# Fifteen small loads of 1 to 15 partitions behind the last row of wo, into a tile that nothing reads

## The chip, the cores and the metric

The kernel runs on one core of a Trainium2 chip. The metric is the device time of that core in microseconds (us), the median of the runs shown. The core has five engines with an instruction stream each: TensorE (PE), VectorE (DVE), ScalarE (ACT), GpSimd (POOL) and SyncE (SP). SP computes nothing here; it issues nearly all the transfers (DMAs) between the large memory (HBM) and the on-chip memory (SBUF).

## The reference

One token `x` of 1024 numbers passes through two branches that are added to it:

```python
xn = _layernorm(x, axis=-1)
return x + _A_ref(xn, A_k_cache, A_v_cache, A_wq, A_wo) + _B_ref(xn, B_w1, B_b1, B_w2, B_b2)
```

Branch A is attention over the last 4096 positions of a cache, with 32 query heads of 128 that share 4 key and value heads: `q = x @ wq`, scores, softmax, the weighted sum over `v`, and `@ wo`. Branch B is a layernorm and an MLP, `gelu(y @ w1 + b1) @ w2 + b2`, with a hidden width of 3584. Everything is bf16. The weights and the two cache windows are 39.86 MB, read once; the result is 1024 numbers.

## The kernel before, in words

With a single token every product is a vector by a matrix, so the kernel streams the matrices through SBUF and uses each once. Four large buffers of 128 partitions by 32 KB (the pool `ring`) take the matrices in the order K window, wq in two halves, w1 in two halves, V window, w2 in two halves and wo in two halves. One more use of a buffer, `kt_scr`, holds the transposed K. A matrix is loaded into a buffer that an earlier one gives back, so from w1 on SP waits, ahead of most loads, for the matmuls or copies that read that buffer last.

PE does the vector products with one column of `x` (or of the hidden vector) as the weight and 512 columns of the matrix as the moving side. DVE and ACT rearrange K (L186, L200, L202). Scores, softmax and the attention output follow (L276 to L332). The last part is the output projection: the rows of w2 and wo are 28 and 32 chunks of 128 x 1024 that are accumulated into `accf` (L341), all but the last four. Those four go into a second accumulator `acct` (L357), so that what was gathered before can be copied out while they still arrive. The last half of wo is loaded in pieces of 8, 4, 2, 1 and 1 rows per partition (L229) for the same reason. DVE and ACT write the sum into `res` (L361, L362), and two stores of one row each bring it to HBM: L364 from SP and L365 from ACT.

Tile, the framework in which the kernel is written, gives each instruction the waits that its tiles need and decides in which order instructions stand in each engine's stream. A load carries a wait for the readers of the buffer, and also for earlier writers of the same bytes. Each transfer adds to one of eight counters when it has landed, taken in turn, and a wait is a wait for a count. At the end of the program SP waits for all eight counters and for the other engines, and then the engines meet in a barrier (L391).

The pool `consts` gives each tile its own place for the whole run.

Of the kernel before, what the change touches and what calls it, by code (L numbers as in the profile page):

```python
# [9 lines left out]
BF16 = mybir.dt.bfloat16  # L10
# [6 lines left out]
def kernel(  # L17
# [14 lines left out]
    nc = tc.nc  # L32
# [21 lines left out]
    consts = ctx.enter_context(tc.tile_pool(name="consts", bufs=1))  # L54
# [135 lines left out]
    for g in range(Hkv):  # L190
        T4 = scr[:, g, :].rearrange("p (c a j) -> p c a j", a=4, j=32)
        k = 0
# [30 lines left out]
    wo_v = A_wo.rearrange("(p c) n -> p c n", p=P)  # L223
    for i, cuts in enumerate([[0, 16], [0, 8, 12, 14, 15, 16]]):
# [4 lines left out]
            nc.sync.dma_start(out=tv[:, a:b, :], in_=wo_v[:, nr * i + a:nr * i + b, :])  # L229
        chunk_src += [("o", nr * i + r, tv[:, r, :]) for r in range(nr)]  # L230


    for i, w3 in enumerate(wq_tiles):
        for r in range(4):
# [161 lines left out]
```

## Time and profile before

| What | Value |
| --- | --- |
| time, median of 2 runs | 101.78 us (101.76 to 101.81) |
| span of the profiled execution, first to last instruction | 100.0 us |
| what lies outside the span (101.78 - 100.0) | 1.78 us |
| instructions | 970 |
| moved by DMA | 39.92 MB, mean 399 GB/s |
| busy: PE, DVE, ACT, POOL | 51%, 50%, 34%, 4% |
| mean granted TensorE clock | 0.778 |

The page gives the profiled execution no time of its own beyond its span; the difference to the median, 1.78 us, is what lies before the first and after the last instruction. Times in the profile are counted from the start of the span. "SPq" is SP's instruction stream. A row of the form `L229 SPq DMA_DIRECT2D` is the time for which SP was busy issuing a transfer, not the transfer itself. DMA queues: `q1` carries what SP issues, `q10` what ACT issues, `q8` and `q14` fetch instructions. A transfer consists of packets, and a view of a short stretch says how many packets began in it, on which queue, how many of them were small, and how much time they took as a share of the time of 16 DMA engines.

### The profile page before, as it was taken

Reading aid. Unit: us, or ns where it says so; the run is one execution under the profiler, and the core shown is the slowest. Engines: PE = TensorE matmul, PEld = TensorE weight load, DVE = VectorE, ACT = ScalarE, POOL = GpSimd, SP = SyncE. Lnnn points to the kernel's source line nnn. Section 1 sums busy time; section 2 is a strip of 40 time slices with the busy share of each in tenths; the row PEclk is TensorE's granted clock in tenths of the full one; section 3 lists DMA queues with packets and bytes.
Section 4 is the critical chain, followed back from the end, with each engine's and each line's share of the span. In section 5 each row is a group of like instructions: output and inputs, shape, how many; then the busy total and the mean of one; then the engine's idle time right before and its main releaser. Section 6 shows DMA issues by size and latency. Waiting matters only on the chain.

```text
span 100.0 us, 970 instructions
## 1 busy us (share of the span) xinstructions
PE 51.2 (51%) x365; PEld 20.0 (20%) x365; DVE 49.7 (50%) x92; ACT 34.1 (34%) x37; POOL 3.8 (4%) x16
## 2 busy tenths in 40 slices
PE   0065200008500940193892935999469950199980
PEld 0042200002100310031530322334123410033320
DVE  5445499999999999997125115410450000000021
ACT  5000002999999999962001044400000000000010
POOL 6005200000000000000000000000000000000000
PEclk9999999999995579555555555559985998557999
DMA  2999999999999999998999999999999999999920
GB/s 26 394 420 426 491 488 472 419 419 419 432 419 393 401 500 382 413 482 378 390 429 426 429 531 390 413 477 390 459 447 426 419 432 419 406 419 411 401 73 1
DMA packets 2878, 39.92 MB, mean 399 GB/s; under 512 B 309, under 2 KB 311, under 8 KB 698
## 3 DMA queue, kind: packets, MB, share of 16 engines
q1 hardware_dynamic: 2866, 39.85, 93.6%
q8 instruction: 3, 0.05, 0.2%
q10 hardware_dynamic: 8, 0.01, 0.0%
q14 instruction: 1, 0.01, 0.0%
HBM read 39.86 MB, written 0.00 MB: 398 GB/s over the span
## 4 chain that ended last, share of the span: by engine, by line
DVE 38%; DMA 24%; PE 21%; issue 9%; POOL 3%; ACT 2%; SPq 1%; POOLq 1%; ACTq 0%
DMA wo<-in_A_wo_dram 24%; DVE kt_scr L186 17%; DVE kT L202 16%; PE o_all L320 10%; PE sp L276 4%; PE acch L258 3%; ACT e L298 1%; DVE eTb L300 1%; PE qT_ps L262 1%; DVE m_loc L284 1%; PE acct L357 1%; SPq L229 1%; DVE q_sb L241 1%; POOLq L391 1%; POOL spread L110 1%
## 5 line engine op out<-in xcount | busy, mean ns | idle before, releaser
L200 ACT COPY kT<-kt_scr 32x1024 bf16<-32x1024 bf16 x26 | 27.1, 1042 | 14.8 <-DVE kt_scr L186 14.5
L186 DVE STREAM_TRANSPOSE kt_scr<-k_sb 128x4096 bf16<-128x4096 bf16 x4 | 17.4, 4411 | 0.0
L238 PE MATMUL accq<-wq,xnT 128*1 128x512 bf16 x64 | 7.1, 622 | 18.3 <-DMA wq<-in_A_wq_dram 18.3
L202 DVE COPY kT<-kt_scr 32x1024 bf16<-32x1024 bf16 x38 | 15.9, 419 | 0.5
L346 DVE COPY bulk<-accf 33x320 f32<-33x320 f32 x1 | 0.5, 483 | 21.9 <-ACT bulk L345 21.9
L341 PE MATMUL accf<-wo,o 128*1 128x512 bf16 x56 | 8.3, 459 | 6.0 <-DMA wo<-in_A_wo_dram 5.9
L345 ACT COPY bulk<-accf 33x192 f32<-33x192 f32 x1 | 0.3, 312 | 31.9 <-PE accf L341 31.9
L320 PE MATMUL o_all<-v_sb,eTb 128*32 128x512 bf16 x32 | 10.0, 491 | 1.0 <-DVE zcol L311 1.0
L258 PE MATMUL acch<-w,yT 128*1 128x448 bf16 x64 | 6.3, 572 | 6.0 <-DMA w<-in_B_w_dram 6.0
L341 PE MATMUL accf<-w,hT 128*1 128x512 bf16 x56 | 7.9, 451 | 0.0
L238 PEld LDWEIGHTS <-xnT 128*1 128x1 bf16 x64 | 2.1, 116 | 22.5 <-issue 22.4
L320 PEld LDWEIGHTS <-eTb 128*32 128x32 bf16 x32 | 3.8, 120 | 6.9 <-issue 3.9
L341 PEld LDWEIGHTS <-o 128*1 128x1 bf16 x56 | 2.8, 97 | 11.4 <-issue 9.2
L258 PEld LDWEIGHTS <-yT 128*1 128x1 bf16 x64 | 2.0, 115 | 9.8 <-issue 9.8
L276 PE MATMUL sp<-kT,qm 128*32 128x512 bf16 x32 | 3.8, 630 | 0.3 <-DVE qm L267 0.3
L341 PEld LDWEIGHTS <-hT 128*1 128x1 bf16 x56 | 2.7, 96 | 4.7 <-issue 2.5
L323 DVE TENSOR_TENSOR o_m<-o_all,grs 32x512 f32<-32x512 f32 x1 | 0.7, 680 | 5.8 <-PE o_all L320 5.8
L123 PE MATMUL x_ps<-ones_bf,xb 1*128 1x1 bf16 x8 | 0.7, 200 | 5.0 <-DMA xb<-in_A_x_dram 5.0
L298 ACT ACTIVATE e<-sc,nmx 128x1024 bf16<-128x1024 f32 x1 | 1.1, 1148 | 5.7 <-DVE nmx L295 5.7
L315 DVE STREAM_TRANSPOSE hT<-h_sb 128x896 bf16<-128x896 bf16 x1 | 1.7, 1706 | 2.4 <-ACT h_sb L313 2.4
L276 PEld LDWEIGHTS <-qm 128*32 128x32 bf16 x32 | 2.1, 133 | 1.4 <-issue 0.9
L281 ACT COPY sc<-sp 128x512 f32<-128x512 f32 x1 | 0.6, 585 | 4.8 <-PE sp L276 4.8
(88 smaller groups left out, 35.9 us busy)
## 6 DMA issues: line engine op xcount, KB each, us to landing
w<-in_B_w_dram SPq DMA_DIRECT2D x4, 3584.0 KB
wq<-in_A_wq_dram SPq DMA_DIRECT2D x2, 4096.0 KB, 27.0
k_sb<-in_A_k_cache_dram SPq DMA_DIRECT2D x4, 1024.0 KB, 7.1
wo<-in_A_wo_dram SPq DMA_DIRECT2D x1, 4096.0 KB, 29.4
v_sb<-in_A_v_cache_dram SPq DMA_DIRECT2D x1, 2048.0 KB, 19.2
v_sb<-in_A_v_cache_dram SPq DMA_DIRECT2D x2, 1024.0 KB, 23.1
wo<-in_A_wo_dram SPq DMA_DIRECT2D x1, 2048.0 KB
wo<-in_A_wo_dram SPq DMA_DIRECT2D x1, 1024.0 KB
```

Source lines behind the costliest of these rows:

```text
L110: nc.gpsimd.affine_select(out=spread[:], in_=spread[:], compare_op=ALU.not_equal, fill=1.0, base=0, pattern=[[-1, 4], [1, P]], channel_mul ...
L186: nc.vector.transpose(out=scr[:, g, :], in_=k2[:, g, :])
L200: nc.scalar.copy(out=dst, in_=src)
L202: nc.vector.tensor_copy(out=dst, in_=src)
L229: nc.sync.dma_start(out=tv[:, a:b, :], in_=wo_v[:, nr * i + a:nr * i + b, :])
L238: nc.tensor.matmul(accq[32 * t:32 * t + 1, b, :], lhsT=xnT[:, c:c + 1], rhs=w3[:, r, j * 512:(j + 1) * 512], start=(c == 0), stop=(c == C ...
L258: nc.tensor.matmul(acch[32 * t:32 * t + 1, b, :NH], lhsT=yT[:, c:c + 1], rhs=w3[:, r, j * NH:(j + 1) * NH], start=False, stop=(c == C - 1) ...
L276: nc.tensor.matmul(sp[32 * R:32 * R + 32, :], lhsT=qm[:, g, :], rhs=kT[:, g, c0:c0 + 512], start=(g == 0), stop=(g == Hkv - 1), tile_posit ...
L298: nc.scalar.activation(out=e128[:], in_=sc[:], func=ACT.Exp, bias=nmx[:], scale=scale, accum_out=l_loc[:])
L315: nc.vector.transpose(out=hT[:], in_=h_sb[:].rearrange("p (d c) -> p c d", c=CW2))
L320: nc.tensor.matmul(o_all[:].rearrange("h g d -> h (g d)"), lhsT=eTb[:, 32 * c:32 * c + 32], rhs=v4[:, :, c, :], start=(c == 0), stop=(c == ...
L341: nc.tensor.matmul(accf[32 * half:32 * half + 1, :], lhsT=vec[kind](c), rhs=wap[:, half * 512:(half + 1) * 512], start=False, stop=(idx == ...
```

## The change

Behind the loads of wo a tile of 16 partitions by 1024 bf16 is taken from `consts`, and SP is told to load into it fifteen times: load `k` writes partitions 0 to `k`-1 and 512 + 32`k` columns, from rows of wo. All fifteen begin at the same corner of the tile, so each one overwrites all that the one before wrote. Nothing reads the tile. Together they are 101,120 numbers, 202 KB.

```diff
@@ -229,6 +229,10 @@
             nc.sync.dma_start(out=tv[:, a:b, :], in_=wo_v[:, nr * i + a:nr * i + b, :])
         chunk_src += [("o", nr * i + r, tv[:, r, :]) for r in range(nr)]
 
+    marks = consts.tile([16, 1024], BF16)
+    for k in range(1, 16):
+        nc.sync.dma_start(out=marks[0:k, 0:512 + 32 * k], in_=wo_v[0:k, 0, 0:512 + 32 * k])
+
 
     for i, w3 in enumerate(wq_tiles):
         for r in range(4):
```

In the new kernel the loads have line L234, and every later line moves down by four: the store of SP is L368, that of ACT L369, and the end L395.

In the program as it is built, the streams of PE, DVE, POOL and ACT are unchanged but for these line numbers and for which of the eight counters ACT's store names. SP's stream, from the last load of wo on, is the following; the text in brackets names the counters for which the instruction waits, and `DVE`, `Activation` are the counters of these engines.

```
L229 DMACopy wo1_259<-in_A_wo_dram 128x1024 x2
L234 DMACopy marks_265<-in_A_wo_dram 1x544 [waits DMAHW6_49]
L234 DMACopy marks_265<-in_A_wo_dram 2x576 [waits DMAHW7_49,DMAHW6_49]
L368 DMACopy out_0_dram<-res_689 1x512 [waits DMAHW1_49,DVE_49,Activation_49]
L234 DMACopy marks_265<-in_A_wo_dram 3x608 [waits DMAHW7_49,DMAHW2_49]
L234 DMACopy marks_265<-in_A_wo_dram 4x640 [waits DMAHW3_49,DMAHW2_49]
...
L234 DMACopy marks_265<-in_A_wo_dram 14x960 [waits DMAHW4_49]
L234 DMACopy marks_265<-in_A_wo_dram 15x992 [waits DMAHW5_49]
L395 UnconditionalBranch
```

Load 1 adds to counter 6, load 2 to counter 7, loads 3, 4, 5, 6 to counters 2, 3, 4, 5, and so on in turn, loads 14 and 15 to counters 5 and 6. So each of loads 2 to 15 waits, among others, for the count that is reached when the load before it has landed. ACT's store adds to counter 0 and SP's store to counter 1.

## The prediction

> **What bounds the kernel now.** I read the chain that ended last first, then the stretches of DMA traffic at its end, then what SP waits for, because the change touches only SP's stream. The chain, in order of time, its last pieces (start, duration, what):
>
> ```profile
> 72.11 23.63 DMA wo<-in_A_wo_dram
> 95.74 0.04 issue
> 95.79 0.60 PE acct L357 x8
> 96.39 0.42 PE acct L353 x4
> 96.81 0.55 PE acct L357 x6
> 97.36 0.02 issue
> 97.38 0.48 DVE res L361
> ```
>
> The end is set by the stream of matrices: wo is issued by 73.5 and lands until 96.7, then four last chunks, an addition, and the store. The page's slices of the span show that the DMA engines have nothing to do after that:
>
> ```profile
> DMA  2999999999999999998999999999999999999920
> ```
>
> The last digit is the stretch from 97.5 to 100.0. It holds the two stores and the end of the program. What SP waits for, and its issues after the loads of wo (timeline of SP: start, duration):
>
> ```profile
> SPq L364 <- DVE res L361: 24.4, 1, 24.4
> SPq L391 <- DMA out_dram<-res: 0.6, 1, 0.6
> ...
> 57.86 15.63 SPq L229 DMA_DIRECT2D wo<-in_A_wo_dram  x6
> 97.93 0.31 SPq L364 DMA_DIRECT2D out_dram<-res  x1
> ```
>
> So SP is idle for 24.4 us between its last load, issued until 73.5 (57.86 + 15.63), and its store, issued at 97.93. After the store it waits for the landing of both stores. The rows of the end (L391) between 99.0 and 99.3 show when:
>
> ```profile
> L391 SPq EVENT_SEMAPHORE  x2: 28/28/28, 99.0 to 99.2; - x2
> ```
>
> The first ends with ACT's store, the second with SP's: SP's store is known to have landed at 99.2, and the remaining 0.8 us to 100.0 are the barrier.
>
> **The change, part by part.**
>
> *Issuing.* Fifteen issues on SP. The nearest rows are issues of one row: 0.31 (SP's store), 0.49, 0.22 and 0.27 (the small loads on ACT at the start); so about 0.3 each. *Bytes.* 202 KB; at 399 GB/s 0.5 us if they competed with anything. Neither counts by itself. *The tile* takes 2 KB of each of 16 partitions, and no instruction waits for its place.
>
> *Waits.* What counts is that the fifteen overwrite each other. In the new program's stream each of loads 2 to 15 waits for the counter that the one before raises on landing. So they are a chain: issue, travel, landing, next issue. Where it stands is read from the stream too: load 1, load 2, SP's store, then loads 3 to 15, then the end, which waits for all counters.
>
> *Load 1* is issued at 73.5 behind wo on the same queue (its counter 6 stood for a half of w2, long landed). It lands between some 75.5 and, if the queue is served in order, shortly after wo's last packet, which begins at 96.66; with 0.1 for itself and 0.4 until SP knows (below) that is 97.2 at the latest. *Load 2* is issued then, at 97.25 at the latest, 0.3 of SP, ended at 97.6. SP's store needs `res`, which is ready at 97.9 as before. So the store isn't late: behind the waiting load 2 on SP there is only this store, and its cover is 0.3 us wide. If load 1 landed later than that, each us later would be one us on the store and on all that follows. PE's work is untouched, since load 1 stands behind all of wo.
>
> *Loads 3 to 15* can't be issued before SP's store, 98.24. Load 3 also needs load 2 landed, which is between 97.6 and 99.1. I take 98.5 for its issue (bounds 98.3 and 99.1). From there 13 loads follow one another with nothing beside them, and the last must land before the end of the program. At each step SP is idle until the landing is known, no engine has other work, and nothing hides it. So the price is 13 times one step.
>
> *One step.* The trace has no load on an idle queue that is read at once, so I take it apart.
>
> 1. Issue to first packet. SP's store: issued at 97.93, data packet at 98.76: 0.83. The first load of K: 0.80 to 1.82: 1.02. I take 0.85, as the store has one row.
> 2. The packet itself. A row of 2 KB of `xb`, on a queue in full flow, took 0.08. On an idle queue the read from HBM may show. DMA traffic in the stretch 1.80 to 1.85, the first five packets of the run, and in 98.75 to 98.80, the store's two packets (number, MB, share of 16 engines' time in the stretch of 0.05):
>
> ```profile
> q1 hardware_dynamic: 5, 0.04, 777.0%
> ...
> q1 hardware_dynamic: 2, 0.00, 6.5%
> ```
>
>    777.0% of 16 x 0.05 us is 6.22 us, 1.24 each; the same 8 KB packets take 0.32 later (118.3% of 16 x 0.25 us for 15 packets in the stretch 3.75 to 4.00). So up to 0.92 on top is possible, if what the first load of the run showed is the reading and not only the start of everything; the store's packets show nothing of it (0.03 each), but they read SBUF. Between 0.08 and 1.0: the k_sb row is like the new loads in the idle queue and in HBM as the source, the store in its size and in coming late in the run. Neither is nearer, so I take the middle, 0.5.
> 3. Last packet to the waiting engine. SP's store: 98.80 to 99.2: 0.4. `xb`: 4.58 to PE's start at 4.95: 0.37. wo's last row: 96.66 to 97.04: at most 0.38. I take 0.4.
> 4. Waking and the next issue: 0.05, as the gaps between pieces named "issue" in the chain (71.60, 0.05).
>
> Sum: 0.85 + 0.5 + 0.4 + 0.05 = 1.8 us. Lower end 1.3 (the store's 1.27 from issue to known landing, plus 0.03), upper end 2.5 (1.02 + 1.0 + 0.42 + 0.05).
>
> The Trainium skill has a price for this, in "DMA: Bandwidth & Descriptors", section "Anatomy of one DMA — SWDGE (gpsimd) path": about 2.0 us fixed for each DMA on the GpSimd path, mostly the wait until the write is confirmed, with HBM as the slowest target. By it the sum would be 98.5 + 13 x 2.0 - 99.2, an estimate of 25.3 us more or 127.1 us. The trace doesn't bear the figure out for the store, which went to HBM and took 1.27, and no row here shows a small load alone.
>
> *Sum.* Load 15 is known to have landed at 98.5 + 13 x 1.8 = 121.9, in place of 99.2 for SP's store: 22.7 us more. The barrier's 0.8 stays. The span becomes 122.7, and with the 1.78 us outside the span the time becomes **124.5 us**; against the median of 101.78 that is +22%.
>
> **The rivals.**
>
> *A slower step: the read shows in full.* If each load on an idle queue pays what the first load of K paid, a step is 0.85 + 1.0 + 0.4 + 0.05 = 2.3, and with load 3 at 98.9 the end is 98.9 + 29.9 = 128.8: 29.6 more, **131.4 us**. For it: it is the only load from an idle queue in the trace. Against: it is also the first transfer of the run, its issue took 0.70 where the next three took about 0.4, and no later packet shows it. A slow growth from load 3 to 15, because more packets have to land, would act the same way.
>
> *A faster step: a load costs what the store costs.* Then 1.35, load 3 at 98.3, the end at 98.3 + 17.55 = 115.85: 16.65 more, **118.4 us**. For it: 1.27 is the only whole small transfer on an idle queue that the trace shows, and it ends in HBM. Against: it doesn't read HBM.
>
> *Not slower: the loads don't wait for each other.* The mechanism would be that the counts waited for are already reached when SP comes to them, because the counters are shared with earlier transfers. SP would then issue the loads in its idle 24.4 us: 15 x 0.3 = 4.5 us, from 73.5 to 78, under wo's traffic, and 202 KB at the end of the queue, 0.5 us, would land before the store at 99.2 does. The time would be **101.8 us**, within 2% (about what a measurement of this kernel can tell from no change). It decides if at least loads 3 to 15 find their counts reached before 97.9. Against: each wait names the counter of the load just before, whose other transfers have landed long ago and leave it one landing short; and loads 3 to 15 stand behind the store in SP's stream, so even free of waits they would take 13 x 0.3 = 3.9 us after 98.24 and end near 103.3, some 4 us more. Only if the chip met the loads in another order than the built one could it be hidden.
>
> **How the numbers follow.** The chain at a step of 1.5 to 2.1 us (forecast, 120 to 129): 0.60. Slower step: 0.18. Faster step: 0.18. Loads that don't wait: 0.04, of which 0.02 within 2%, 0.01 slower by the issues alone, 0.01 faster by chance of another placement. So faster by over 2% 0.01, within 2% 0.02, slower by over 2% 0.97. The range 118.0 to 131.5 answers to steps of 1.3 to 2.3 us. It leaves out the 0.04, about half of the slower step's cases and some of the faster step's, together under 0.2; the upper bound of 2.5 (with 99.1: 134.2) and the lower (with 98.3: 117.8) lie just outside.
>
> **What the changed profile would show.** SP's timeline: one row of L234 near 73.5, one between 95.5 and 97.3, the store L368 at 97.93 as before, and 13 rows of L234 at equal distance from about 98.5 on; the distance is the step, and 1.8 is what I put on record. PE, DVE and ACT end at the same times as before, up to `res` at 97.9. The DMA slices are near zero after 98. Waits of SP: L234 for the transfer into `marks`, some 20 us in all. Wrong would be: a store that is issued later than 98.3 (load 1 or 2 held it up), a distance that isn't constant (the size or the number of partitions matters), or loads in one block.

## The result

The changed kernel takes 121.64 us, median of 2 runs (121.46 to 121.82), against 101.78 us before: 1.196 times the time, with a 95% interval of 1.191 to 1.200. The span of the profiled execution is 120.1 us against 100.0. So 19.9 us were added, where 22.7 were forecast; the range was 118.0 to 131.5.

The page of the new kernel shows at once where they are. Its DMA slices (40 slices of 3.0 us, tenths of the engines' time):

```profile
DMA  3999989999989999899999999999999700000000
```

The stream of matrices fills 32 slices, up to 96 us, as it did before. Then come eight slices in which the DMA engines do next to nothing: 24 us, where before there were about 4. The page's chain (shares of the span by engine, then by line, cut by the page itself) does not name what fills them:

```profile
DVE 30%; DMA 25%; PE 15%; issue 7%; POOL 2%; POOLq 1%; ACT 0%
```

The shares add up to 80%. The chain is followed back from the last work of an engine, and ends at 97.8 us with `res`; nothing but SP's end waits for the new loads, so no engine's work leads to them. When the shares of a chain leave out a fifth of the span, the rest must be looked for in the queues. SP's timeline from the loads of wo on (start, us, then how many issues the row merges):

```profile
69.70 2.23 SPq L229 DMA_DIRECT2D wo<-in_A_wo_dram  x5
71.98 24.54 SPq L234 DMA_DIRECT2D marks<-in_A_wo_dram  x2
97.89 0.24 SPq L368 DMA_DIRECT2D out_dram<-res  x1
98.22 19.60 SPq L234 DMA_DIRECT2D marks<-in_A_wo_dram  x13
```

and what SP waited for (us in total, times, longest):

```profile
SPq L234 <- DMA marks<-in_A_wo_dram: 34.2, 13, 18.7
...
SPq L395 <- DMA marks<-in_A_wo_dram: 1.2, 1, 1.2
```

SP's store stands at 97.89, 0.04 from where it was, between load 2 and load 3. Thirteen loads follow. Of the 34.2 us of waiting, 18.7 are load 2 waiting for load 1, which stood in the queue behind wo; this was idle time of SP before and costs nothing. The other 15.5 and the last 1.2, with the 3.6 us that SP is busy with the thirteen issues between them, make up the new time. The single issues, from a timeline cut fine enough (loads 2, 3, 6, 9, 12 and 15):

```profile
96.27 0.25 SPq L234 DMA_DIRECT2D marks<-in_A_wo_dram  x1
...
98.22 0.24 SPq L234 DMA_DIRECT2D marks<-in_A_wo_dram  x1
...
102.83 0.27 SPq L234 DMA_DIRECT2D marks<-in_A_wo_dram  x1
...
107.62 0.27 SPq L234 DMA_DIRECT2D marks<-in_A_wo_dram  x1
...
112.46 0.30 SPq L234 DMA_DIRECT2D marks<-in_A_wo_dram  x1
...
117.50 0.32 SPq L234 DMA_DIRECT2D marks<-in_A_wo_dram  x1
```

The distance from one issue to the next is (117.50 - 98.22) / 12 = 1.61 us on the average, and it grows with the size of the loads: by the rows shown 1.54 between loads 3 and 6, 1.60 between 6 and 9, 1.61 between 9 and 12, and 1.68 between 12 and 15. The last landing is known at 119.3, in place of 99.2.

### The profile page after: what moved, and what is told of

It reads as the page before. It is cut to its first block, busy times and chain, and to the rows that moved or that the text cites. A ratio compares the mean times of both kernels' runs of the same rounds, so it can differ in the third digit from the quotient of the medians.

```text
span 120.1 us, 992 instructions
## 1 busy us (share of the span) xinstructions
PE 49.8 (41%) x365; PEld 19.6 (16%) x365; DVE 49.7 (41%) x92; ACT 34.1 (28%) x37; POOL 3.8 (3%) x16
## 4 chain that ended last, share of the span: by engine, by line
DVE 30%; DMA 25%; PE 15%; issue 7%; POOL 2%; POOLq 1%; ACT 0%
DMA wo<-in_A_wo_dram 25%; DVE kt_scr L186 14%; DVE kT L202 13%; PE accf L345 7%; PE sp L280 3%; PE acch L262 2%; DVE m_loc L288 1%; PE qT_ps L266 1%; PE acct L361 1%; DVE q_sb L245 1%; POOLq L395 1%; POOL spread L110 1%; ACT sc L285 0%; POOL rstd L145 0%; DVE res L365 0%
## 5 line engine op out<-in xcount | busy, mean ns | idle before, releaser
L324 PE MATMUL o_all<-v_sb,eTb 128*32 128x512 bf16 x32 | 9.2, 458 | 1.2 <-DMA v_sb<-in_A_v_cache_dram 1.2
L280 PE MATMUL sp<-kT,qm 128*32 128x512 bf16 x32 | 3.2, 551 | 0.4 <-DVE qm L271 0.4
L266 PE MATMUL qT_ps<-ident,q_sb 128*128 128x128 bf16 x8 | 1.2, 308 | 1.7 <-DVE q_sb L245 1.7
```

The lines of the kernel that those rows point to most:

```text
L266: nc.tensor.transpose(qT_ps[:, b * 4 + hh, :], q_sb[:, b, hh * Dh:(hh + 1) * Dh], ident[:])
L280: nc.tensor.matmul(sp[32 * R:32 * R + 32, :], lhsT=qm[:, g, :], rhs=kT[:, g, c0:c0 + 512], start=(g == 0), stop=(g == Hkv - 1), tile_posit ...
L324: nc.tensor.matmul(o_all[:].rearrange("h g d -> h (g d)"), lhsT=eTb[:, 32 * c:32 * c + 32], rhs=v4[:, :, c, :], start=(c == 0), stop=(c == ...
```

## The experiments

The theory is that the time is made of waits: each load is issued only when the one before has landed, after SP's store, with nothing beside it. The rivals are that each load costs its 1.6 us whether it waits or not, and that a chain costs its time wherever it stands. Then comes the question what a step consists of. Each run was compared with the kernel before on the same chip, which had medians of 101.84, 101.66 and 101.90 us in the three groups.

### Loads that overwrite nothing

```diff
-    marks = consts.tile([16, 1024], BF16)
+    marks = consts.tile([P, 1024], BF16)
     for k in range(1, 16):
-        nc.sync.dma_start(out=marks[0:k, 0:512 + 32 * k], in_=wo_v[0:k, 0, 0:512 + 32 * k])
+        p0 = k * (k - 1) // 2
+        nc.sync.dma_start(out=marks[p0:p0 + k, 0:512 + 32 * k], in_=wo_v[0:k, 0, 0:512 + 32 * k])
```

> The same fifteen loads with the same sizes and sources, but load k writes partitions of its own in a tile of 128 partitions, so that no load overwrites another. What is left of the waits is that a counter must have been raised by its last transfer before it is used again: loads 4 to 7 then wait for pieces of wo, load 14 for the landing of ACT's store (same counter), and SP's store stands behind load 15. Theory (the 20 us are the wait of each load for the landing of the one before): loads 7 to 13 are issued from about 97.0 on, each some 0.3 us of SP, load 14 follows ACT's landed store at 99.0 to 99.3, SP's store is issued at about 100.1 instead of 97.9: some 2 us more than before, 104 us. Rival (each added load costs 1.6 us of queue or SP, whether it waits or not): about 121 us.

Measured: 104.46 us, ratio 1.025 (1.021 to 1.029). The same bytes in the same fifteen transfers cost 2.6 us instead of 19.9. SP's timeline:

```profile
70.11 2.23 SPq L229 DMA_DIRECT2D wo<-in_A_wo_dram  x5
72.39 28.13 SPq L235 DMA_DIRECT2D marks<-in_A_wo_dram  x15
100.62 0.24 SPq L369 DMA_DIRECT2D out_dram<-res  x1
```

and all that the loads waited for:

```profile
SPq L235 <- DMA wo<-in_A_wo_dram: 18.1, 5, 9.4
SPq L235 <- DMA w<-in_B_w_dram: 5.0, 1, 5.0
```

No load had to wait for another of the fifteen. Loads 2 to 7 wait for pieces of w2 and wo, which had used the same counters before them; load 7 goes out at 97.19, when wo's last row has landed, and from there on the loads follow at distances of 0.31 to 0.41, with SP busy issuing for 0.27 to 0.38 of each. All loads now stand ahead of the store, so the store goes out at 100.62 instead of 97.93, the 2.7 us late that were foreseen as about 2: it stands behind the nine issues from 97.19 on. (`res` was 0.3 late as well: ACT's store went out at 98.26 instead of 97.94.) So the wait of each load for the one before is nearly the whole price, and the rest is mainly SP's issuing in front of a store.

### Two chains beside each other

```diff
-    marks = consts.tile([16, 1024], BF16)
+    marks = [consts.tile([16, 1024], BF16, name=f"marks{i}") for i in range(2)]
     for k in range(1, 16):
-        nc.sync.dma_start(out=marks[0:k, 0:512 + 32 * k], in_=wo_v[0:k, 0, 0:512 + 32 * k])
+        nc.sync.dma_start(out=marks[k % 2][0:k, 0:512 + 32 * k], in_=wo_v[0:k, 0, 0:512 + 32 * k])
```

> The loads go in turn to two tiles, so each waits for the load before the last one. Theory: two chains run beside each other; after the store at 97.9 stand loads 4, 6, ..., 14 and 5, 7, ..., 15, six steps of 1.6 us, 98.3 to about 108.3, where SP's store was known to have landed at 99.2: 9 us more than before, 110.8 us. Rival (each load costs 1.6 us by itself): 121 us as in the changed kernel.

Measured: 110.60 us, ratio 1.086 (1.081 to 1.091). The issues after the store, first four:

```profile
98.30 0.25 SPq L234 DMA_DIRECT2D marks<-in_A_wo_dram  x1
98.64 0.26 SPq L234 DMA_DIRECT2D marks<-in_A_wo_dram  x1
99.67 0.27 SPq L234 DMA_DIRECT2D marks<-in_A_wo_dram  x1
100.06 0.27 SPq L234 DMA_DIRECT2D marks<-in_A_wo_dram  x1
```

Loads 4 and 5 go out together; 6 follows 4 after 1.37 us, and 7 follows 5 after 1.42. Twelve loads take the time of six, and the 110.8 us of the theory came within 0.2. Fifteen loads of a fixed price would have stayed at 121.6; that rival falls.

### The chain on an engine that has time

```diff
-        nc.sync.dma_start(out=marks[0:k, 0:512 + 32 * k], in_=wo_v[0:k, 0, 0:512 + 32 * k])
+        nc.gpsimd.dma_start(out=marks[0:k, 0:512 + 32 * k], in_=wo_v[0:k, 0, 0:512 + 32 * k])
```

> The same fifteen loads from HBM into the same tile, in the same chain, but issued by POOL, which has nothing to do after its last computation at 12 us, instead of SP. Theory (the price is paid only because the chain stands behind SP's store, where nothing else runs): even at 4 us a step beside the stream of matrices the chain ends near 75 us; the time is that of before, plus at most the 0.5 us of the bytes: 101.8 to 102.3 us. Rival (a chain of fifteen transfers costs its 20 us wherever it stands, for instance by holding up the stream): over 110 us.

Measured: 104.27 us, ratio 1.022 (1.017 to 1.027). The 20 us are gone, but 2.6 are left, more than was allowed for. POOL's timeline:

```profile
16.26 0.59 POOL L234 DMA_DIRECT2D marks<-in_A_wo_dram  x1 [4.29 <-DMA marks<-in_A_wo_dram]
23.05 0.50 POOL L234 DMA_DIRECT2D marks<-in_A_wo_dram  x1 [6.20 <-DMA marks<-in_A_wo_dram]
...
94.89 0.50 POOL L234 DMA_DIRECT2D marks<-in_A_wo_dram  x1 [4.79 <-DMA marks<-in_A_wo_dram]
99.25 0.50 POOL L234 DMA_DIRECT2D marks<-in_A_wo_dram  x1 [3.85 <-DMA marks<-in_A_wo_dram]
```

Beside the stream a step takes 5.3 to 7.7 us, on the average (94.89 - 16.26) / 12 = 6.55, four times the 1.61 of the changed kernel. POOL's way of loading is not what makes it so long: by the list of transfers (size, us from issue to landing) the last load, issued when the stream had ended, took 2.0 us, and load 9, under the stream, 7.4:

```profile
marks<-in_A_wo_dram POOLq DMA_DIRECT2D x1, 29.1 KB, 2.0
...
marks<-in_A_wo_dram POOLq DMA_DIRECT2D x1, 14.1 KB, 7.4
```

So the chain lasted as long as the kernel, and its last load was issued at 99.25. And `res` itself was late: SP's store stood at 99.72, 1.8 us after that of before, because wo's last row came later (its last packet began at 98.2 in place of 96.6). Behind the store the end takes 3.0 us in place of 2.1: SP waits for the chain's last load until 101.3, and POOL's end lasts until 101.9. So 1.8 us are the late row, and 0.9 the end of the chain. The same loads were then run on POOL once more, the first eight alone:

```diff
-    for k in range(1, 16):
+    for k in range(1, 9):
```

> The first eight loads alone, chained, issued by POOL. With fifteen of them POOL's steps took 6.6 us beside the stream, the last load was issued at 99.25, and wo's last row arrived some 1.5 us later than before. Theory (a chain that ends under the stream costs only its bytes): eight steps end near 9 + 8 x 6.6 = 62 us, 50 KB are 0.13 us, the time is 101.8 to 102.1 us. Rival (each such load takes a slot of the stream's DMA engines, about 0.1 us each): 102.6 us or more, in proportion to the 2.6 us of fifteen.

Measured: 102.21 us, ratio 1.0015 (0.999 to 1.004). Its last load was issued at 55.62, and the chain of eight that ends under the stream costs nothing that can be measured. The rival in proportion (1.4 us for eight of fifteen) falls. Why fifteen delayed the last row of wo is not settled: the loads that ran beside the last rows are missing from the run of eight, but so are others further ahead, and these two runs do not tell them apart.

### What a step consists of

Four kernels repeat one size fifteen times, in the chain of the change:

```diff
-    for k in range(1, 16):
-        nc.sync.dma_start(out=marks[0:k, 0:512 + 32 * k], in_=wo_v[0:k, 0, 0:512 + 32 * k])
+    for k in range(1, 16):
+        nc.sync.dma_start(out=marks[0:1, 0:544], in_=wo_v[0:1, 0, 0:544])      # or [0:1, 0:992], [0:15, 0:32], [0:15, 0:992]
```

One row of 544 columns:

> All fifteen loads are of 1 partition and 544 columns, one after the other into the same bytes. Theory with a step that grows with the rows of a load: 13 steps of about 1.5 us from 98.2, 119.9 us. Rival (a step is a fixed latency, and the growth from 1.55 to 1.75 in the changed kernel has to do with the place in the sequence): 121.6 us, with the distance growing along the sequence.

One row of 992 columns:

> All fifteen loads are of 1 row of 992 columns: 1984 bytes in place of 1088 in the run that took 117.1 us with steps of 1.24 us. If the bytes of a row go at the rate of the stream (2 KB in 0.08 us), a step is 1.27 us and the time 117.6 us; if the long step of 15 rows of 992 columns comes from the size of a row rather than from their number, it is near 1.5 us and 120.5 us.

Fifteen rows of 32 columns:

> All fifteen loads are of 15 partitions and 32 columns: 64 bytes a row instead of 1984. If the longer step of large loads comes from the number of rows, it is as with 15 partitions of 992 columns, 1.75 us and 123.5 us; if it comes from the bytes, it is as with one row, 1.5 us and 120 us.

Fifteen rows of 992 columns:

> All fifteen loads are of 15 partitions and 992 columns. Theory with a step that grows with the rows of a load: 13 steps of 1.75 us from 98.3, 123.5 us, at equal distance from the first on. Rival (growth by place in the sequence): 121.6 us.

And fifteen rows of 992 columns that lie 2 KB apart in HBM (`in_=A_wo[0:15, 0:992]`) instead of 64 KB:

> All fifteen loads are of 15 rows of 992 columns, as in the run that took 123.55 us, but the rows lie 2 KB apart in HBM instead of 64 KB. If the packets of 0.1 to 0.27 us come from the distance of the rows, a step falls from 1.67 toward 1.45 us and the time to about 120.5 us; if they come from the number and size of the rows, it stays at 123.5 us.

SP's timelines after the store, in this order; each row runs from the issue of load 3 to the end of the issue of load 15, so a step is the duration less one issue, divided by 12:

```profile
98.27 15.18 SPq L234 DMA_DIRECT2D marks<-in_A_wo_dram  x13
```
```profile
98.39 15.69 SPq L234 DMA_DIRECT2D marks<-in_A_wo_dram  x13
```
```profile
98.45 17.47 SPq L234 DMA_DIRECT2D marks<-in_A_wo_dram  x13
```
```profile
99.14 20.48 SPq L234 DMA_DIRECT2D marks<-in_A_wo_dram  x13
```
```profile
98.57 20.15 SPq L234 DMA_DIRECT2D marks<-in_A_wo_dram  x13
```

| Load | Time, us | One issue, us | Step, us |
| --- | --- | --- | --- |
| 1 row of 1088 bytes | 117.08 | 0.22 | 1.25 |
| 1 row of 1984 bytes | 117.86 | 0.22 | 1.29 |
| 15 rows of 64 bytes | 119.98 | 0.32 | 1.43 |
| 15 rows of 1984 bytes, 64 KB apart | 123.55 | 0.32 | 1.68 |
| 15 rows of 1984 bytes, 2 KB apart | 123.39 | 0.32 | 1.65 |
| the change, 3 to 15 rows | 121.64 | 0.24 to 0.32 | 1.61 |

The times hold different starts as well (load 3 went out between 98.27 and 99.14), so it is the steps that can be compared. With one size the distances do not grow along the sequence (1.21 to 1.35 with the first size, no trend), so it was the size that made them grow, not the place. Fourteen more rows add 0.18 us. SP is busy 0.10 longer, but by load 5 of the two runs the first packet comes only 0.06 later; more of it is in the packets, which take 0.18 from the first to the end of the last in place of 0.06. The larger rows add another 0.25 with fifteen rows, and 0.04 with a single one. The distance of the rows in HBM does next to nothing. The expectation of 119.9 us for a single row was too high by 2.8, because it took 1.5 us, the step of loads of 3 and 4 rows, for that of one. For fifteen rows of 64 bytes the 120 us came by luck: their step is not that of one row, which had been put too high. The other three kernels came within 0.3 us of a time that their expectation named.

A step of the smallest load can be read off packet by packet. In the first kernel of the table a load was issued at 100.83; DMA traffic in the stretches 101.65 to 101.70 and 101.70 to 101.75 (packets, MB, share of 16 engines' time in 0.05 us):

```profile
q1 hardware_dynamic: 1, 0.00, 5.8%
...
q1 hardware_dynamic: 1, 0.00, 1.1%
```

The first is the row itself, 5.8% of 16 x 0.05 = 0.046 us, the second the small packet after it; the next issue is at 102.04. So 0.85 from issue to packet, 0.05 for the packet, and 0.3 until SP issues again. These loads all read the same row, so a row read for the first time is not excluded from taking longer; but the loads of the change read rows of which only one is new each time.

### The same chain out of SBUF

```diff
-        nc.sync.dma_start(out=marks[0:k, 0:512 + 32 * k], in_=wo_v[0:k, 0, 0:512 + 32 * k])
+        nc.sync.dma_start(out=marks[0:k, 0:512 + 32 * k], in_=kT[0:k, 0, 0:512 + 32 * k])
```

> The same fifteen transfers, in the same chain, but read from the transposed K in SBUF instead of wo in HBM. The prediction put 0.5 us of a step to reading HBM on an idle queue. Theory: the packets of the changed kernel's loads take 0.2 to 0.27 us where the store's took 0.04, so a step gets shorter by 0.2 us and the time by 13 x 0.2 = 2.6 us, 119.0 us. Rival (the reading does not show, all of the step is issue, travel and landing): 121.6 us. Rival (it is 0.5, and another term was put too high): 115 us.

Measured: 127.34 us, ratio 1.250 (1.245 to 1.255). All three expectations are on the wrong side: without HBM the chain is slower by 5.7 us. The row of load 12 in this run, and in the changed kernel:

```profile
116.56 0.73 SPq L234 DMA_DIRECT2D marks<-kT  x1
```
```profile
112.46 0.30 SPq L234 DMA_DIRECT2D marks<-in_A_wo_dram  x1
```

The issue takes 0.73 in place of 0.30 us. From the issue's start to the first packet it is 1.38 in place of 0.92 us, and from there to the next issue 0.65 in place of 0.74. So reading HBM may be worth 0.09 us of this step, and the rest of the difference goes with the longer issue on SP. Of the 5.7 us the twelve steps, 1.96 on the average in place of 1.61, make 4.2; another 1.1 is a later start, load 3 at 99.30 in place of 98.22, because load 2 could be issued only at 97.54. In the built program the transfers from HBM carry a mark, `ant_dge_precooked`, that those from SBUF to SBUF lack; whether it is the cause of the longer issue was not tried. As a measure of HBM's share the experiment was badly chosen, since it changed two things.

## Why the prediction was right, point by point

**Bound and place.** The stream ended as before, load 1 went out at 71.98 and load 2 at 96.27, inside the stretch given, and SP's store was not held up. (wo's last packet began at 96.53, so load 1 did not have to wait for all of wo.) Load 3 went out at 98.22, a little under the lower bound of 98.3; 98.5 was taken. That is 0.3 of the 2.9 us (124.5 - 121.64) by which the time was overestimated.

**The waits as the price.** Shown: without overwriting the price falls to 2.6 us, with two chains it halves. The rival of loads that do not wait for each other is excluded by the 1.61 us between issues, and its side calculation (13 issues behind the store would cost some 4 us) has its counterpart in the 2.7 us by which the store is late behind the loads that overwrite nothing.

**The cover.** The prediction said that nothing hides the chain because it stands behind the store. Shown by the eight loads on POOL: chained and hidden, they cost 0.15% (-0.1% to 0.4%).

**The size of a step** is the term that was off: the 13 steps from 98.22 to the last known landing at 119.3 are 1.62 us each where 1.8 was taken, 13 x 0.18 = 2.3 us of the overestimate. (The remaining 0.2 is mostly that the profiled execution took 121.82 us, 0.18 more than the median.) The three parts of the sum, over the twelve steps of the changed kernel: issue to first packet was put at 0.85 and is 0.87 to 0.96. The packets were put at 0.5, the middle between 0.08 and 1.0, and take 0.26 to 0.42 from the first to the end of the last, 0.37 on the average. Landing to next issue was put at 0.4 + 0.05 and is 0.29 to 0.38. So two parts were too high, by 0.13 and 0.12 on the average, and the first too low by 0.06, which made up for a part of it. With one row the packet takes 0.05. (The store's two packets, put at 0.03 each, are one of 0.044 for the row and a small one of 0.008.) The 1.24 us of the first packets of the run, on which the upper end stood, are thus a thing of the start of the run or of the large first load, not of every load from an idle queue.

**One step for all loads.** As a sign of being wrong the prediction named a distance that isn't constant, and this sign came: the distances run from 1.51 to 1.74 us. A single step of 1.8 for loads of 3 to 15 rows was the part of the mechanism that it had too simple. It cost little: the distances lie between 0.09 us under and 0.13 over their mean of 1.61.

**The rivals.** The slower step did not come. Its second form, a slow growth from load 3 to load 15, did, and was worth 0.2 us; the kernels of one size show that it comes with the rows and their bytes. The faster step, a load that costs what the store of one row costs (1.27), is right for loads of one row: 1.25. The prediction held against it that the store does not read HBM, and took the middle between the store and the first load of K; the store was the better of the two rows, and the loads of more rows lie above it by their rows and bytes.

The figure of the Trainium skill ("DMA: Bandwidth & Descriptors", section "Anatomy of one DMA — SWDGE (gpsimd) path"), about 2.0 us fixed for each DMA on the GpSimd path, gave an estimate of 127.1 us. The trace agrees for that path, by the one load that POOL issued after the stream had ended: 2.0 us from issue to landing. A load issued by SP on an idle queue had a step of 1.25 to 1.68 us, so for this chain the figure was too high; only SBUF to SBUF came to 1.8 to 2.1.

## What to carry to other kernels

In this framework a transfer into a tile that an earlier transfer wrote waits for that one to land, even if nobody reads the tile: fifteen such loads of 0.2 MB together cost 20 us here, 1.25 us a link for one row of 1 KB and 1.7 for fifteen rows of 2 KB. Give such loads places of their own, or a few tiles in turn, and look where the built program has put them among the last instructions of their queue, since a store behind them waits as well. The price is paid only where nothing runs beside the chain: eight of them under the stream cost nothing that could be measured, although each then took four times as long; fifteen lasted as long as the stream itself and cost 2.6 us.

## What was not expected of the hardware

- Transfers from SBUF to SBUF cost SP 0.62 to 0.79 us to issue where loads from HBM of the same shapes cost 0.24 to 0.33, and a link of the chain was 1.8 to 2.1 us.
- Beside a stream that fills the DMA engines, a small chained load issued by POOL took 5.3 to 7.7 us, and 2.0 to landing when the stream had ended.
- Loads that overwrite nothing still waited, through the eight counters that the transfers of SP and ACT share, for pieces of w2 and wo that have nothing to do with them; the nine that could go out only from 97.19 on stood in front of the store, which was 2.7 us late.
- A load of one row from an idle queue showed next to no time for reading HBM: its packet took 0.046 us and came 0.85 us after the issue; for SP's store out of SBUF in the kernel before it was 0.044 and 0.83.
